# Attention output copied out of PSUM by one ScalarE operation per half head, with GpSimd moving the parts between partitions

## The chip, the cores and the metric

The kernel runs on one core of a Trainium2 chip. The metric is the device time of one execution in microseconds (us). Five engines matter: TensorE (PE in the profile, with its weight loads as a row of their own, PEld), VectorE (DVE), ScalarE (ACT), GpSimd (POOL), and SyncE (SP), which issues most of the DMAs. Each of them works through its own list of instructions in the order in which the program was built; an instruction that waits for a semaphore holds up all that stands behind it on its engine.

## The reference

A clustered attention over 2 batches, 8 heads, 768 positions and head dimension 64, followed by two layers of the form x @ w_in, an elementwise function, @ w_out:

```python
mask = q_assign[:, :, :, None] == k_assign[:, :, None, :]
scores = scale * np.matmul(q, k.transpose(0, 1, 3, 2))
scores = np.where(mask, scores, -1000000000.0)
scores = scores - np.max(scores, axis=-1, keepdims=True)
attn = np.exp(scores)
attn = attn / (np.sum(attn, axis=-1, keepdims=True) + 1e-09)
return np.matmul(attn, v).astype(np.float32)
...
x = np.ascontiguousarray(attn_out.transpose(0, 2, 1, 3)).reshape(B * S, H * D)
h = x @ w_in          # first layer: g = h * cos(h)
return (g @ w_out)    # the second layer has a piecewise quadratic in place of h * cos(h)
```

`q_assign` and `k_assign` are the index of the nearest of 16 centroids per head.

## The kernel before

All matrix products are made from two parts per operand, a rounded high part and the remainder, so that products keep nearly full fp32 accuracy. The work has two stages.

**Attention (to about 285 us).** There are 8 pairs (a batch and two neighbouring heads). A pair has four units (i, h, hf): head h of the pair, half hf of the 768 queries; they run in the order h0 hf0, h0 hf1, h1 hf0, h1 hf1. A unit has six slots. In each slot PE transposes a 128-row piece of the probabilities (`p_transpose`, L499, into one of three PSUM banks with the tag "t"), ACT copies it as its high part `phi` (L502), DVE subtracts for the low part `plo` (L507), PE makes scores eight slots ahead (L453, L456), DVE takes the row maximum `nm` (L462), ACT the exponential `p` (L471), and PE multiplies phi and plo with the values (`p_v`, L517 and L518) into `o`, the only PSUM bank of its kind. `o` holds 128 partitions: 64 of the product with the high part of V, 64 of that with the low part.

When a unit's sixth product is issued, `o_parts` follows: ACT copies the half of `o` that is called main into the tile `xt0` and the other half into `xt1` (L531, two operations of 64 x 384). Both heads of a pair share these two tiles, on 64 partitions each. After a unit with h = 1, `finish` follows two slots later: PE transposes the reciprocals `rb` of the softmax sums into a bank `r` (L541, tag "t" too), GpSimd adds xt0 and xt1 (L543), DVE multiplies the sum by r (L544), and GpSimd makes the two parts `xh` (L547) and `xl` (L551) that the layers read. So each pair has two finishes, one for each hf; below they are called the first and the second finish of a pair.

`inverse` makes the reciprocals of a unit: GpSimd adds a small number to `den` (L481), DVE inverts (L482), and GpSimd spreads each of three columns over 64 columns of `rb` (L486, three operations that multiply a tile `ones` by the column).

Beside this runs `prep_pair`, which prepares the pair after the next in small steps between slots: transposes of q and k (L322), their parts on GpSimd (L294, L295), products with the centroids (`pd`), the assignment to a centroid on DVE and GpSimd (`eq` L382 on DVE, times `desc` L383 on GpSimd, `mx` L388 and `dots` L390 on DVE), the two parts of V (`vv`, L403 and L404 on GpSimd), a transpose of `dots` on PE (`po`, L410, tag "t"), and its copy `oht` on ACT (L430). Its end falls beside the second finish of pairs 0 to 5.

**The two layers (from about 285 us).** PE runs long products (L652 to L654); the other engines apply the elementwise functions and split the weights into parts (`convert_chunk`, L144 to L160).

What sets the order: functions are put off by a number of slots with `later`, and a scheduler then places the instructions of each engine; the order on an engine is fixed when the kernel is built.

## Time and profile before

| what | value |
|---|---|
| time, median of 3 runs | 826.47 us (824.32 to 827.69) |
| the profiled execution's own time | 821.31 us |
| its span | 819.5 us |
| PE, DVE, ACT, POOL busy | 97%, 77%, 51%, 33% of the span |
| granted TensorE clock | 1.00 (full speed) |

The span is what the instructions cover; 1.8 us of the execution lie around it. PE is busy nearly all of the span, but its records overlap, so a busy PE is not a PE at its peak; waits are read from the idle time ahead of single instructions. A row of the timeline gives the start, the length, the engine, the line, what is written from what, the shape, a count where neighbours are merged, and in square brackets the idle time of the engine before it and what ended it.

### The profile page before, as it was taken

To read this page: it belongs to the slowest core of one execution; us is meant where nothing else is said; L and a number is where in the kernel's file an instruction comes from. 1 tells how busy PE (TensorE), PEld (TensorE's weight loads), DVE (VectorE), ACT (ScalarE), POOL (GpSimd) and SP (SyncE) were. 2 spreads that over 40 slices of the span, in tenths; PEclk is the share of its full clock that TensorE was granted. 3 is DMA by queue.
4 is the path that set the end of the run, shared out by engine and by line. 5 is a ranking of instruction groups with operands and counts; after the bars stand their busy time and mean duration, and the time that the engine had idled before them with its cause. 6 is when DMAs were issued, how large, how long until landed. Compare 5 with 4: busy or idle time off the path is not lost.

```text
span 819.5 us, 11332 instructions
## 1 busy us (share of the span) xinstructions
PE 798.6 (97%) x4042; PEld 665.8 (81%) x4043; DVE 633.6 (77%) x957; ACT 417.1 (51%) x794; POOL 270.4 (33%) x442
## 2 busy tenths in 40 slices
PE   7899999999999999999999999999999999999998
PEld 4788888988888887888888888888888888888886
DVE  5779899899898686787878778887876987755552
ACT  3788888897889764444343424223434233222220
POOL 3356655577553241222211211442231122111110
PEclk9999999999999999999999999999999999999999
DMA  7847556446540002222131222121122121000012
GB/s 145 192 89 155 142 121 166 101 107 137 137 89 33 1 15 89 102 70 85 51 104 52 103 58 97 52 88 67 52 59 96 56 89 62 1 1 0 14 50 92
DMA packets 48183, 65.97 MB, mean 80 GB/s; under 512 B 27904, under 2 KB 32640, under 8 KB 48128
## 3 DMA queue, kind: packets, MB, share of 16 engines
q1 hardware_dynamic: 46432, 64.83, 29.0%
q10 hardware_dynamic: 1696, 0.43, 0.3%
q8 instruction: 32, 0.52, 0.3%
q14 instruction: 23, 0.19, 0.1%
HBM read 43.02 MB, written 3.15 MB: 56 GB/s over the span
## 4 chain that ended last, share of the span: by engine, by line
PE 62%; DVE 1%; ACT 1%; POOL 1%; issue 0%; POOLq 0%
PE y L654 11%; PE y L653 11%; PE y L652 11%; PE h L653 10%; PE h L654 10%; PE h L652 10%; DVE gl L614 0%; DVE r L622 0%; POOL gh L610 0%; DVE g L627 0%; ACT L623 0%; ACT r L623 0%; DVE w L160 0%; ACT n L621 0%; ACT wx L144 0%
## 5 line engine op out<-in xcount | busy, mean ns | idle before, releaser
L610 POOL TENSOR_SCALAR gh<-g 128x512 fp32r<-128x512 f32 x96 | 70.8, 738 | 292.4 <-DVE g L641 165.3
L653 PE MATMUL h<-xl,w 128*128 128x512 f32 x384 | 151.5, 395 | 0.0
L652 PE MATMUL h<-xh,w 128*128 128x512 f32 x384 | 151.5, 395 | 0.0
L654 PE MATMUL h<-xh,w 128*128 128x512 f32 x384 | 151.4, 394 | 0.0
L507 DVE TENSOR_TENSOR plo<-pt,phi 128x384 fp32r<-128x384 f32 x192 | 99.8, 548 | 16.9 <-ACT phi L502 15.6
L502 ACT ACTIVATE phi<-pt 128x384 fp32r<-128x384 f32 x192 | 91.2, 493 | 21.0 <-PE pt L499 19.1
L637 ACT ACTIVATE p<-h,mone 128x512 f32<-128x512 f32 x48 | 33.0, 688 | 134.4 <-DVE m L636 134.0
L499 PE MATMUL pt<-ident,p 128*128 128x128 f32 x576 | 96.7, 278 | 4.3 <-DVE plo L507 2.8
L462 DVE TENSOR_REDUCE nm<-s 128x1 f32<-128x768 f32 x96 | 90.7, 946 | 6.9 <-PE s L456 6.3
L471 ACT ACTIVATE p<-s,nm 128x768 f32<-128x768 f32 x96 | 86.8, 904 | 12.8 <-DVE nm L462 12.5
L614 DVE TENSOR_TENSOR gl<-g,gh 128x512 fp32r<-128x512 f32 x96 | 71.1, 741 | 20.0 <-POOL gh L610 15.0
L654 PEld LDWEIGHTS h<-xh,w 128*128 128x128 f32 x384 | 71.9, 187 | 17.6
L653 PEld LDWEIGHTS h<-xl,w 128*128 128x128 f32 x384 | 71.9, 187 | 17.5
L652 PEld LDWEIGHTS h<-xh,w 128*128 128x128 f32 x384 | 71.9, 187 | 17.5
L144 ACT ACTIVATE wx<-wraw 128x1024 f32<-128x1024 f32 x32 | 36.4, 1138 | 95.6 <-DMA wraw<-in_moe_w_in_dram 35.8
L453 PE MATMUL s<-st,st 128*128 128x384 f32 x192 | 78.7, 411 | 4.2 <-ACT p L471 3.6
L499 PEld LDWEIGHTS pt<-ident,p 128*128 128x128 f32 x576 | 69.2, 140 | 15.1 <-DVE plo L507 3.1
L654 PE MATMUL y<-gh,w 128*128 128x512 f32 x192 | 74.9, 390 | 1.2 <-DVE w L160 1.2
L691 DVE TENSOR_TENSOR acc<-y,acc 128x512 f32<-128x512 f32 x72 | 49.3, 685 | 33.5 <-PE y L654 33.5
L653 PE MATMUL y<-gl,w 128*128 128x512 f32 x192 | 74.9, 390 | 0.0
L653 PE MATMUL y<-w,gh 128*128 128x512 f32 x192 | 74.9, 390 | 0.0
L652 PE MATMUL y<-gh,w 128*128 128x512 f32 x192 | 74.8, 390 | 0.0
(118 smaller groups left out, 1641.7 us busy)
## 6 DMA issues: line engine op xcount, KB each, us to landing
wraw<-in_moe_w_in_dram SPq DMA_DIRECT2D x16, 1024.0 KB, 5.2
wraw<-in_moe_w_out_dram SPq DMA_DIRECT2D x16, 1024.0 KB, 4.9
st<-t SPq DMA_DIRECT2D x24, 192.0 KB, 4.4
st<-th SPq DMA_DIRECT2D x9, 384.0 KB, 3.9
st<-tl SPq DMA_DIRECT2D x18, 192.0 KB, 4.1
st<-th SPq DMA_DIRECT2D x18, 192.0 KB, 4.2
nat<-in_q_dram SPq DMA_DIRECT2D x8, 384.0 KB, 5.3
natv<-in_v_dram SPq DMA_DIRECT2D x8, 384.0 KB, 4.7
```

The source lines that it names most:

```text
L453: nc.tensor.matmul(s[:, step, :HS], qt[:, 0, cols], kt[:, 0, kc], start=True, stop=False)
L462: nc.vector.tensor_reduce(nm, s[:, :, :HS], AX.XY, ALU.max, negate=True)
L471: nc.scalar.activation(p, s[:, :, :HS], AF.Exp, bias=nm, accum_out=dens[u][:, jj, 0:1])
L499: nc.tensor.transpose(ps[:, jj * P:(jj + 1) * P], p[:, kt * P:(kt + 1) * P], ident)
L502: nc.scalar.activation(hi, ps, AF.Copy)
L507: nc.vector.tensor_tensor(lo, ps, hi.bitcast(F32), ALU.subtract)
L610: nc.gpsimd.tensor_scalar(hi, g, 1.0, 0.0, ALU.mult, ALU.add)
L614: nc.vector.tensor_tensor(lo, g, hi.bitcast(F32), ALU.subtract)
L652: nc.tensor.matmul(o, lh, rh, start=first, stop=False)
L653: nc.tensor.matmul(o, lh, rl, start=False, stop=False)
L654: nc.tensor.matmul(o, ll, rh, start=False, stop=last)
L691: nc.vector.tensor_tensor(a, po, a, ALU.add)
```

## The change

`o_parts` copies the whole of `o`, 128 x 384, in one ACT operation into a tile of its own, `xt0` for h = 0 and `xt1` for h = 1. The parts of the two heads then lie on opposite partitions. After the second head, three GpSimd operations of 64 x 384 bring them together: one takes partitions 64 to 127 of head 0's tile to partitions 0 to 63 of a third tile `xt2`, one takes partitions 0 to 63 of head 1's tile to partitions 64 to 127 of `xt2`, and one takes partitions 0 to 63 of head 0's tile to the same partitions of head 1's tile. The sum in `finish` then reads `xt1` and `xt2`. `inverse` writes all three columns in one GpSimd operation, 128 x 192, from a broadcast of `den`, and the tile `ones` is gone.

```diff
-            for jj in range(HJ):
-                nc.gpsimd.tensor_scalar(rb[(i, hf)][:, jj, h], ones, den[:, jj, 1:2], 1.0,
-                                        ALU.mult, ALU.mult)
+            nc.gpsimd.tensor_scalar(
+                rb[(i, hf)][:, :, h], den[:, :, 1].unsqueeze(2).to_broadcast([P, HJ, D]),
+                1.0, 0.0, ALU.mult, ALU.add)
...
-            if h == 0:
-                xt[(i, hf)] = [ap.tile([P, HS], F32, tag=f"xt{n}", bufs=2,
-                                       name=f"xt{n}_{i}_{hf}") for n in range(2)]
-            for t, rows in zip(xt[(i, hf)], (main, other)):
-                nc.scalar.activation(t[main], o[rows], AF.Copy)
+
+            t = ap.tile([P, HS], F32, tag=f"xt{h}", bufs=2, name=f"xt{h}_{i}_{hf}")
+            xt.setdefault((i, hf), []).append(t)
+            nc.scalar.activation(t, o, AF.Copy)
             if h == 1:
+                t0 = xt[(i, hf)][0]
+                t2 = ap.tile([P, HS], F32, tag="xt2", bufs=1, name=f"xt2_{i}_{hf}")
+                xt[(i, hf)] = (t, t2)
+                for dst, rows, src in ((t2, main, t), (t2, other, t0), (t, other, t0)):
+                    src = src[rows] if dst is t else src[main if rows is other else other]
+                    nc.gpsimd.tensor_scalar(dst[rows], src, 1.0, 0.0, ALU.mult, ALU.add)
                 later(2, finish, i, hf)
```

The scheduler places the new operations. GpSimd's list around the second finish of pair 2 before the change, from the end of the first finish (`xl`) on; `vv` are the parts of V of the pair that is being prepared, and the row that adds two `xt` tiles is the sum of this finish:

```order
L551 TENSOR_TENSOR xl<-xt_2_0_1592,xh 128x384
L383 TENSOR_TENSOR eq_1909<-eq_1909,desc 128x384
L403 TENSOR_SCALAR vv_2037<-natv_1526 128x6x64 x2
L404 TENSOR_TENSOR vv_2037<-natv_1526,vv_2037 128x6x64
L543 TENSOR_TENSOR xt_2_1_1713<-xt_2_1_1713,xt_2_1_1714 128x384
L404 TENSOR_TENSOR vv_2037<-natv_1526,vv_2037 128x6x64
L481 TENSOR_SCALAR den_1944<-den_1944 128x3
```

and the same place with the change (the line numbers differ there: L535 are the three copies, L546 is the sum, and L381, L401 and L402 are L383, L403 and L404 of before):

```order
L554 TENSOR_TENSOR xl<-xt_2_0_1835,xh 128x384
L535 TENSOR_SCALAR xt_2_1_1961<-xt_2_1_1695 64x384
L381 TENSOR_TENSOR eq_1891<-eq_1891,desc 128x384
L401 TENSOR_SCALAR vv_2019<-natv_1512 128x6x64 x2
L535 TENSOR_SCALAR xt_2_1_1961<-xt_2_1_1959 64x384
L402 TENSOR_TENSOR vv_2019<-natv_1512,vv_2019 128x6x64
L535 TENSOR_SCALAR xt_2_1_1959<-xt_2_1_1695 64x384
L402 TENSOR_TENSOR vv_2019<-natv_1512,vv_2019 128x6x64
L546 TENSOR_TENSOR xt_2_1_1959<-xt_2_1_1959,xt_2_1_1961 128x384
L479 TENSOR_SCALAR den_1924<-den_1924 128x3
```

One copy stands ahead of `eq`, two stand between the `vv` operations, and the sum moved behind the second low part of V. The second finishes of pairs 0 and 3 read like this one. In pairs 4 and 5 the two high parts of V stand ahead of `eq`, in both kernels, and the rest is the same. In pair 1 the sum stood behind both low parts of V already, and only the copies come ahead of it.

DVE's list at the same place, with the change:

```order
L505 TENSOR_TENSOR plo_3_1970<-pt_3_1965,phi_3_1969 128x384
L505 TENSOR_TENSOR plo_4_1982<-pt_4_1977,phi_4_1981 128x384
L547 TENSOR_TENSOR xt_2_1_1961<-xt_2_1_1959,r_1_1996 128x384
L388 TENSOR_TENSOR dots_1789<-eq_1891,mx_1890 128x384
L480 RECIPROCAL den_1924<-den_1924 128x3
L460 TENSOR_REDUCE nm_2040<-s_1984 128x1
```

Nothing moved here: before the change the same operations stand in the same places (DVE's row 207 is the product of this finish in both), `dots` right behind the product `xt<-xt,r`.

## Rows read from the trace of the kernel before

**Rows 1.** One stretch: busy us (instructions) of PE, PEld, DVE, ACT, POOL; clock, DMA.

```profile
125.00:165.00 40.00, 38.76 (x265) 35.80 (x265) 35.52 (x62) 33.03 (x74) 24.31 (x45) 1.00 0.54 126
```

**Rows 2.** Groups by line and shape: busy us, mean ns | idle before, releaser.

```profile
L531 ACT ACTIVATE xt<-o 64x384 f32<-64x384 f32 x64 | 31.0, 484 | 2.9 <-PE o L518 2.1
...
L330 ACT ACTIVATE t<-ptq 128x384 f32<-128x384 f32 x24 | 11.9, 495 | 0.6 <-PE ptq L322 0.4
...
L486 POOL TENSOR_SCALAR rb<-ones,den 128x64 f32<-128x64 f32 x96 | 30.1, 332 | 5.6 <-DVE den L482 5.6
...
L305 POOL TENSOR_SCALAR st<-th 64x768 fp32r<-64x768 f32 x2 | 1.7, 828 | 0.2
```

**Rows 3.** Waits from 40 to 285 us: who for whom, us, times, longest.

```profile
PEld o L517 <- ACT xt L531: 6.9, 16, 0.7
...
PE o L517 <- ACT xt L531: 2.2, 7, 0.4
```

**Rows 4.** Timeline of GpSimd, second finish of pair 2.

```profile
131.27 1.00 POOL L383 TENSOR_TENSOR eq<-eq,desc 128x384 f32<-128x384 f32 x1 [0.49 <-DVE eq L382]
132.24 0.99 POOL L403 TENSOR_SCALAR vv<-natv 128x384 fp32r<-128x384 f32 x2
133.20 1.01 POOL L404 TENSOR_TENSOR vv<-natv,vv 128x384 fp32r<-128x384 f32 x1
134.18 1.01 POOL L543 TENSOR_TENSOR xt<-xt,xt 128x384 f32<-128x384 f32 x1
135.15 1.01 POOL L404 TENSOR_TENSOR vv<-natv,vv 128x384 fp32r<-128x384 f32 x1
```

**Rows 5.** DVE and PE there: the product, `dots`, and `po` that reads it.

```profile
135.22 0.56 DVE L544 TENSOR_TENSOR xt<-xt,r 128x384 f32<-128x384 f32 x1
135.69 0.88 DVE L390 TENSOR_TENSOR dots<-eq,mx 128x384 f32<-128x384 f32 x1
...
136.75 0.50 PE L410 MATMUL po<-ident,dots 128*128 128x128 f32 x3
...
139.27 0.44 PE L453 MATMUL s<-st,st 128*128 128x384 f32 x1 [0.21 <-ACT p L471]
```

**Rows 6.** Second finish of pair 1: GpSimd's sum, DVE, PE.

```profile
101.11 1.01 POOL L543 TENSOR_TENSOR xt<-xt,xt 128x384 f32<-128x384 f32 x1
...
102.16 0.56 DVE L544 TENSOR_TENSOR xt<-xt,r 128x384 f32<-128x384 f32 x1 [0.78 <-POOL xt L543]
102.63 0.55 DVE L390 TENSOR_TENSOR dots<-eq,mx 128x384 f32<-128x384 f32 x1
...
103.32 0.52 PE L410 MATMUL po<-ident,dots 128*128 128x128 f32 x3 [0.29 <-DVE den L482]
...
105.87 0.44 PE L453 MATMUL s<-st,st 128*128 128x384 f32 x1 [0.21 <-ACT p L471]
```

**Rows 7.** Second finish of pair 4: GpSimd's sum, DVE's product, `po`.

```profile
199.26 1.00 POOL L543 TENSOR_TENSOR xt<-xt,xt 128x384 f32<-128x384 f32 x1
...
200.63 0.54 DVE L544 TENSOR_TENSOR xt<-xt,r 128x384 f32<-128x384 f32 x1
...
202.43 0.49 PE L410 MATMUL po<-ident,dots 128*128 128x128 f32 x3
```

**Rows 8.** First finish of pair 2, and PE's wait ahead of the second.

```profile
124.73 1.00 POOL L543 TENSOR_TENSOR xt<-xt,xt 128x384 f32<-128x384 f32 x1 [2.89 <-ACT xt L531]
...
127.78 0.54 DVE L544 TENSOR_TENSOR xt<-xt,r 128x384 f32<-128x384 f32 x1
...
132.46 0.44 PE L517 MATMUL o<-phi,vv 128*128 128x384 f32 x1 [0.39 <-ACT xt L531]
```

**Rows 9.** The end of attention: the last finish, then the first layer's first ACT.

```profile
284.40 0.98 ACT L531 ACTIVATE xt<-o 64x384 f32<-64x384 f32 x2 [1.12 <-PE o L518]
...
285.46 1.02 POOL L543 TENSOR_TENSOR xt<-xt,xt 128x384 f32<-128x384 f32 x1 [0.70 <-ACT xt L531]
...
288.81 0.60 ACT L621 ACTIVATE n<-h 128x512 int32<-128x512 f32 x1 [3.42 <-POOL xl L551]
```

More of the change, by code (lines that the diff above doesn't have):

```diff
@@ L74, in attention_moe_moe @@
         nc.gpsimd.memset(desc[:, c:c + 1], float(C - c))
-    ones = cpool.tile([P, D], F32, name="ones")
-    nc.gpsimd.memset(ones, 1.0)
     ohscale = cpool.tile([P, 1], F32, name="ohscale")
```

## The prediction, made blind

> **What bounds the kernel now.** I read the busy times by stretch first, then the waits, then the timeline around the copies, and last the chain of waits at the end of attention. From 125 to 165 us PE is busy 38.76 of 40 us [rows 1], so in the attention stage PE sets the pace and all that another engine can give back is PE's idle time: 1.24 us in 40, some 7.6 us from 40 to 285 us. DVE and ACT, at 35.5 and 33.0 of 40, are close behind, and each of the two stalls PE now and then. The two layers behind attention are not touched by the edit. So the question is which of PE's waits the edit takes away, and whether it puts others in their place.
>
> The wait that the edit aims at is there: PE's next product into `o` waits for ACT to have copied `o` out, 16 times for 6.9 us on the weight load ahead of it, of which 2.2 us in 7 cases show as idle time of the matmuls themselves [rows 3]. At 132.46 us PE sat idle 0.39 us for it [rows 8].
>
> A second thing matters more. GpSimd's sum (L543) at the second finish of a pair is followed by DVE's product (L544) almost at once: the sum of pair 2 ends at 134.18 + 1.01 = 135.19 us [rows 4], the product starts at 135.22 [rows 5]. DVE had just come to it, so nothing is lost today, but nothing is left either. Behind the product on DVE stands `dots`, and PE's transpose `po` waits for `dots`: it starts at 136.75, 0.18 us after `dots` ends. PE works its list in order.
>
> **What ACT gives back.** 64 copies of 0.484 us go; 32 copies of 128 x 384 come, which I price by the same shape copied from PSUM at L330, 0.495 us [rows 2]. ACT is relieved of 31.0 - 15.8 = 15.2 us, and `o` is free 0.49 us sooner per unit. By the paragraph above that is worth between 0 and 7.6 us, since PE cannot gain more than it idles. The waits named for these copies are the nearer rows: 2.2 us as seen on the matmuls, 6.9 us on the loads. Part of them lies between `eq` and `po` of a second finish, as the one at 132.46 does; there the GpSimd chain below sets when `po` runs, and an earlier `o` only makes PE wait longer for it. I take 2.5 us, a little above what the matmuls show, because ACT's exponentials behind a copy come sooner too.
>
> **What GpSimd gets.** The broadcast of the reciprocals: 96 operations of 0.332 us go, 32 of 128 x 192 come. I have no row of that shape; 128 x 64 takes 0.33 us and 128 x 384 about 0.50 us (two in 0.99 us, [rows 4]), so it lies between, some 0.35 us, and each unit frees some 0.6 us of GpSimd. This is off the path. What it hides is the copy that now stands ahead of `eq`: that copy fits in that 0.6 us plus the 0.49 us for which GpSimd waited there [rows 4], so `eq` does not move. Without that cover it would cost another 0.5 us per second finish.
>
> The copies: 48 of 64 x 384. No copy between partitions on GpSimd is in the trace. An operation over 64 partitions takes 0.83 us for 768 columns [rows 2], one over 128 partitions 0.50 us for 384 [rows 4], so the count of columns sets the time and not that of partitions, and a copy takes 0.50 us; below it could be 0.33 us, as for 64 columns [rows 2], above 1.0 us, as for two-input work of 384 columns [rows 4]. I take 0.50 us, from the row of the same columns.
>
> **First finishes.** Two copies stand ahead of the sum: +1.0 us, and 0.1 us for each of the two waits of one GpSimd operation for the one before (an estimate, from the 0.08 us by which the sum of the last finish starts after ACT's end at 285.38 [rows 9]), less the 0.49 us by which ACT is sooner: +0.7 us. The sum of pair 2 ends at 125.73 and DVE's product starts at 127.78 [rows 8], so 2.05 us are left there; GpSimd had idled 2.89 us before. Hidden.
>
> **Second finishes of pairs 0, 2, 3.** Between `eq` and the sum GpSimd now has two copies more (2 x 0.50) and the second low part of V, which before stood behind the sum (0.98 us, from 133.20 to 134.18 [rows 4]): +1.98 us. DVE's place for the product has not moved, and the 0.03 us of slack are kept as the delay of the signal. So the product of pair 2 starts at 137.20 in place of 135.22, and DVE stands idle in front of it for about 2 us with `dots`, the reciprocal, the next `nm` and `plo` behind it. How `po` follows when PE is already waiting is seen in pair 1, where both low parts of V are ahead of the sum today: DVE idles 0.78 us for the sum, PE idles 0.29 us, and `po` starts 103.32 - 102.16 = 1.16 us after the product [rows 6]. Then `po` of pair 2 starts at 138.36 in place of 136.75: +1.6 us. Three pairs: 4.8 us.
>
> **Pair 1.** Only the copies come in, each now followed at once by one that needs its result: 1.0 us and 0.2 us for these waits. DVE waits already, so all of it is added: 1.2 us.
>
> **Pairs 4 and 5.** The same +1.98 us on GpSimd; its sum of pair 4 ends at 200.26, DVE came at 200.63 [rows 7], so the product moves to 200.26 + 1.98 + 0.03 = 202.27, and `po` to 203.43 from 202.43: +1.0 us. Pair 5 reads alike. Together 2.0 us.
>
> **Where it goes.** Is that stall made good later? From `po` to the next place where PE waits for ACT's exponential it is 2.52 us in pair 2, where `po` did not wait (136.75 to 139.27 [rows 5]), and 2.55 us in pair 1, where it did (103.32 to 105.87 [rows 6]). The pipeline starts from `po` alike in both cases; the delay is carried on whole. Loss at second finishes: 4.8 + 1.2 + 2.0 = 8.0 us.
>
> The Trainium skill, "SBUF — State Buffer", section Who interferes with whom, says that a DVE operation with two SBUF inputs and a GpSimd operation that reads SBUF shut each other out for the whole instruction. `dots` took 0.88 us beside a low part of V and 0.55 us alone [rows 4 to 6]; blocked to 136.16 it would have ended at 136.71, and it ended at 136.57, so the trace agrees nearly. With the change no GpSimd work is left beside `dots`, which is why 1.16 us (pair 1) and not 1.53 us (pair 2) is the distance that I use; by the latter the loss would be 1.1 us larger in the first three.
>
> **The end.** The last finish has no cover: ACT ends 0.49 us sooner, but three copies come ahead of the sum, one of them behind `xl` of the finish before: the sum starts about 1.1 us later than 285.46, and the first layer's `n` on ACT, which waits for the last `xl` [rows 9], with it. The chain that ended last runs through this `n`. +1.0 us.
>
> **Sum.** 8.0 - 2.5 + 1.0 = +6.5 us: 827.8 us for an execution like the profiled one (821.31 us). That execution is 0.6% below the median of the runs, 826.47 us; against the median I say 833.0 us, 0.8% more. A measurement of this kernel can tell some 0.5%, 4.1 us, from no change.
>
> **The rivals.**
> *The stall is swallowed.* DVE comes to its product later than today for another reason, or the ACT time given back shortens PE's two waits behind `po`, so that half the 8.0 us is regained. For it: DVE and ACT are both nearly full. Against it: the equal distances in pairs 1 and 2. It decides once DVE arrives over 1 us later than today. 4.0 - 2.5 + 1.0 = +2.5 us, 829.0 us: no change to tell.
> *The edit does what it is for.* The gain is the 6.9 us of the loads and GpSimd's extra work finds cover everywhere, at +1.0 us at the end: -5.9 us, 820.6 us, faster. It needs the product to stand 2 us later on DVE than it does today, and the list of DVE is unchanged there. Against it also that some of the 6.9 us lies beside matmuls that still ran.
> *The copies cost double*, 1.0 us each, like two-input work: then 2 x 0.5 us more at six second finishes, 1.5 us more at the end: +6.5 + 7.5 = +14, 840.5 us. Against it the rows for one input. The Trainium skill, "GPSIMD Engine Reference", section Engine selection, advises against GpSimd for elementwise work, about half as fast as DVE for two inputs, but near line rate for one; the rows for one and for two inputs, 0.50 and 1.0 us, agree with that.
>
> **How the numbers follow.** Forecast 0.60, swallowed 0.20, what it is for 0.10, double 0.10. The forecast's own spread: copies of 0.33 us take some 2 us off, a gain of 6 us in place of 2.5 takes 3.5 off, a gain of nothing adds 2.5; so 829 to 837 us, and some 0.07 of its 0.60 ends within 0.5% of before. Slower 0.63, same 0.26, faster 0.11. The range reaches from inside the second case to just short of the double price: 825.5 to 838.5 us, with about 0.1 out on either side.
>
> **What would show it.** Right: an idle time of DVE of 1.6 to 2 us before its product at six places, ended by GpSimd's sum; `po` on PE waiting for DVE over 1 us at the same six; the wait of PE for the copy of `o` much smaller; GpSimd's copies at 0.5 us; the first layer starting some 6 us later. Wrong: if DVE's idle time there is short, or if PE's idle time elsewhere in the stage shrinks by as much as `po` adds. Then attention ends as early as before and the edit is worth nothing or a gain.

## The result, and the profile after

The changed kernel takes 832.96 us (median of 4 runs, 832.28 to 837.25) against 825.39 us for the kernel before on the same chip (823.11 to 827.69). The ratio is 1.011 with a 95% interval of 1.008 to 1.0141: slower by 6.6 to 11.6 us, 9.1 us in the middle (the two medians are 7.6 us apart). The forecast was 833.0 us.

The profiled execution took 833.6 us, 12.3 us more than the one of before. I split its span at two marks in both traces: the end of the last `o` matmul of the first unit, and that of the last unit.

| stretch | before | after | difference |
|---|---|---|---|
| start, to the end of the first unit | 39.69 us | 43.57 us | +3.9 |
| attention, first to last unit | 244.68 us | 251.45 us | +6.8 |
| the two layers, to the end of the span | 535.13 us | 536.78 us | +1.65 |

The first of the three isn't the edit's. A stretch's row has its length, then busy us (instructions) of PE, PEld, DVE, ACT, POOL, the granted clock, DMA share and GB/s:

```profile
9.60:19.80 10.20, 10.20 (x40) 7.60 (x40) 6.21 (x16) 0.98 (x2) 4.75 (x5) 0.50 0.99 192
214.40:217.80 3.40, 3.40 (x16) 3.27 (x15) 2.77 (x5) 2.99 (x9) 0.36 (x2) 0.50 0.28 74
```

From 9.6 to 19.8 us TensorE ran at half its clock, the 1.2 GHz level. In the profiled execution of before it ran at 1.00 there. The kernel with the broadcast alone, below, has the same stretch at 0.50, its first unit ends at 43.43 us, and its time is that of the kernel before. So about 8.4 us of the profile's difference are the edit's. The second row is another such drop, inside attention; it comes back at the end.

In attention PE is no longer full. The stretch of [rows 1], with the edit:

```profile
125.00:165.00 40.00, 36.71 (x257) 34.29 (x256) 32.81 (x59) 29.60 (x66) 23.48 (x38) 1.00 0.65 149
```

PE 36.71 us in place of 38.76, ACT 29.60 in place of 33.03. The new operations, by line and shape (busy us, mean ns | idle before, releaser), cost what was put down for them:

```profile
L535 POOL TENSOR_SCALAR xt<-xt 64x384 f32<-64x384 f32 x48 | 25.3, 527 | 55.9 <-ACT xt L528 53.7
...
L528 ACT ACTIVATE xt<-o 128x384 f32<-128x384 f32 x32 | 15.9, 497 | 2.4 <-PE o L516 2.3
L483 POOL TENSOR_SCALAR rb<-den 128x192 f32<-128x192 f32 x32 | 11.3, 354 | 9.3 <-DVE den L480 9.3
```

ACT's copies went from 31.0 us [rows 2] to 15.9. And the waits from 40 to 292 us (us, times, longest) show both sides of the edit at once:

```profile
DVE xt L547 <- POOL xt L546: 15.3, 8, 2.6
...
PE po L408 <- DVE den L480: 10.3, 6, 1.9
...
PEld o L515 <- ACT xt L528: 1.5, 6, 0.4
...
PE o L515 <- ACT xt L528: 0.3, 1, 0.3
```

The wait that the edit aimed at fell from 6.9 us on the loads and 2.2 us on the matmuls [rows 3] to 1.5 and 0.3. In its place PE waits 10.3 us for `po`, in six places, where it waited 0.29 us once [rows 6]. The rows name `den` for it, because DVE's reciprocal of `den`, right behind `dots`, is what ended last before `po` started; what `po` reads is `dots`.

One such place, GpSimd at the second finish of pair 2, to be held beside [rows 4]:

```profile
135.97 1.01 POOL L381 TENSOR_TENSOR eq<-eq,desc 128x384 f32<-128x384 f32 x1
136.94 0.99 POOL L401 TENSOR_SCALAR vv<-natv 128x384 fp32r<-128x384 f32 x2
138.02 0.51 POOL L535 TENSOR_SCALAR xt<-xt 64x384 f32<-64x384 f32 x1
138.61 1.01 POOL L402 TENSOR_TENSOR vv<-natv,vv 128x384 fp32r<-128x384 f32 x1
139.59 0.51 POOL L535 TENSOR_SCALAR xt<-xt 64x384 f32<-64x384 f32 x1
140.07 1.00 POOL L402 TENSOR_TENSOR vv<-natv,vv 128x384 fp32r<-128x384 f32 x1
141.04 0.99 POOL L546 TENSOR_TENSOR xt<-xt,xt 128x384 f32<-128x384 f32 x1
```

GpSimd idles nowhere here for more than 0.1 us; the sum simply stands at the end of its list and starts 5.07 us after `eq`, where it was 2.91. DVE and PE at the same place, beside [rows 5]:

```profile
138.55 1.01 DVE L505 TENSOR_TENSOR plo<-pt,phi 128x384 fp32r<-128x384 f32 x2
142.06 0.55 DVE L547 TENSOR_TENSOR xt<-xt,r 128x384 f32<-128x384 f32 x1 [2.50 <-POOL xt L546]
142.54 0.55 DVE L388 TENSOR_TENSOR dots<-eq,mx 128x384 f32<-128x384 f32 x1
...
143.23 0.52 PE L408 MATMUL po<-ident,dots 128*128 128x128 f32 x3 [1.85 <-DVE den L480]
...
145.78 0.44 PE L451 MATMUL s<-st,st 128*128 128x384 f32 x1 [0.21 <-ACT p L469]
```

DVE comes to the product at 139.56 us and stands 2.50 us; `dots`, which has nothing to do with the sum, stands behind it; `po` follows 1.17 us after the product; 2.55 us later PE waits 0.21 us for ACT, exactly as before. Pair 1 and pair 4, beside [rows 6] and [rows 7]:

```profile
108.05 0.55 DVE L547 TENSOR_TENSOR xt<-xt,r 128x384 f32<-128x384 f32 x1 [2.61 <-POOL xt L546]
...
109.22 0.52 PE L408 MATMUL po<-ident,dots 128*128 128x128 f32 x3 [1.82 <-DVE den L480]
...
211.65 0.56 DVE L547 TENSOR_TENSOR xt<-xt,r 128x384 f32<-128x384 f32 x1 [1.76 <-POOL xt L546]
...
212.82 0.52 PE L408 MATMUL po<-ident,dots 128*128 128x128 f32 x3 [1.44 <-DVE den L480]
```

At a first finish, beside [rows 8], the same copies cost nothing: the sum is over at 131.29 us, and DVE comes to the product at 132.65 without having waited.

```profile
129.09 1.10 POOL L535 TENSOR_SCALAR xt<-xt 64x384 f32<-64x384 f32 x2 [2.90 <-ACT xt L528]
130.27 1.02 POOL L546 TENSOR_TENSOR xt<-xt,xt 128x384 f32<-128x384 f32 x1
...
132.65 0.54 DVE L547 TENSOR_TENSOR xt<-xt,r 128x384 f32<-128x384 f32 x1
```

The end of attention, beside [rows 9]: three copies between ACT's and the sum.

```profile
295.12 0.49 ACT L528 ACTIVATE xt<-o 128x384 f32<-128x384 f32 x1 [1.78 <-PE o L516]
295.84 1.69 POOL L535 TENSOR_SCALAR xt<-xt 64x384 f32<-64x384 f32 x3
297.62 1.02 POOL L546 TENSOR_TENSOR xt<-xt,xt 128x384 f32<-128x384 f32 x1
...
300.98 0.60 ACT L624 ACTIVATE n<-h 128x512 int32<-128x512 f32 x1 [5.36 <-PE h L657]
```

From the end of the last `o` matmul (295.02 us) to the first layer's `n` it is 5.96 us; before it was 288.81 - 284.37 = 4.44 us. PE doesn't stand still for this, as it has products of the first layer to run. It meets the delay once, at a product of the second layer that waits for the weight part `w`, which DVE makes 19 us behind `n` in both kernels; this is the only wait of its matmuls behind attention, before and after:

```profile
309.41 0.50 PE L654 MATMUL y<-gh,w 128*128 128x512 f32 x1 [1.17 <-DVE w L160]
...
321.76 0.50 PE L657 MATMUL y<-gh,w 128*128 128x512 f32 x1 [2.17 <-DVE w L158]
```

That is 1.0 of the 1.65 us. The rest is work on the other side of the mark: three of the first layer's products `h`, some 0.23 us each, ran ahead of the last `o` product before and run behind it now.

### The profile page after: what moved, and what is told of

It is laid out like the page before. It is cut to its first block, busy times and chain, and to the rows that moved or that the text cites. A ratio compares the mean times of both kernels' runs of the same rounds, so it can differ in the third digit from the quotient of the medians.

```text
span 831.8 us, 11292 instructions
## 1 busy us (share of the span) xinstructions
PE 800.6 (96%) x4043; PEld 671.0 (81%) x4043; DVE 631.3 (76%) x957; ACT 400.1 (48%) x762; POOL 278.0 (33%) x425
## 4 chain that ended last, share of the span: by engine, by line
PE 80%; DVE 5%; POOL 5%; ACT 4%; issue 3%; DMA 2%; SPq 1%; ACTq 0%; POOLq 0%; DVEq 0%
PE y L657 10%; PE y L656 10%; PE y L655 10%; PE h L657 10%; PE h L656 10%; PE h L655 10%; PE pt L497 5%; PE s L451 3%; PE s L454 2%; PE o L515 2%; PE o L516 2%; DVE plo L505 1%; POOL vv L402 1%; ACT p L469 1%; PE pd L351 1%
## 5 line engine op out<-in xcount | busy, mean ns | idle before, releaser
L500 ACT ACTIVATE phi<-pt 128x384 fp32r<-128x384 f32 x192 | 92.9, 501 | 28.4 <-PE pt L497 26.4
L656 PE MATMUL y<-w,gh 128*128 128x512 f32 x192 | 74.8, 390 | 0.0
L655 PE MATMUL y<-w,gh 128*128 128x512 f32 x192 | 74.7, 389 | 0.0
```

The source lines that it names most:

```text
L500: nc.scalar.activation(hi, ps, AF.Copy)
L655: nc.tensor.matmul(o, lh, rh, start=first, stop=False)
L656: nc.tensor.matmul(o, lh, rl, start=False, stop=False)
```

## The experiments

The theory: the loss is the *place* of the copies in GpSimd's list, ahead of a sum for which DVE waits with `dots` and so `po` behind it; ACT's shorter copy is a true gain beside it. The rivals, by the letters that the expectations use: A, ACT's 128-row form or the broadcast costs; B, the stalls are swallowed and the difference is the start's clock; C, the GpSimd work itself costs, wherever it stands; D, any time that DVE stands still ends up on PE. "In us" below is the ratio's excess times the median of the kernel before in the same comparison.

One number is taken from every trace: PE's time in the **six stretches** that hold a second finish beside a preparation, each from the end of one unit's last `o` matmul to that of the next, and in the rest of attention.

| kernel (one profiled execution each) | six stretches | rest of attention | ratio, 95% interval |
|---|---|---|---|
| before | 48.65 us | 196.03 us | 1 |
| changed | 57.93 | 193.52 | 1.011, 1.008 to 1.0141 |
| broadcast alone | 48.00 | 196.80 | 0.9999, 0.9981 to 1.0016 |
| GpSimd copies alone | 53.37 | 197.52 | 1.0076, 1.0053 to 1.0099 |
| one late copy more | 60.88 | 194.57 | 1.0173, 1.0141 to 1.0205 |
| product put off | 63.91 | 205.37 | 1.0354, 1.0317 to 1.039 |
| `dots` first | 54.75 | 195.13 | 1.0051, 1.0032 to 1.007 |
| head 0 alone | 48.11 | 195.00 | 0.9985, 0.9965 to 1.0004 |
| head 0 alone, V parts behind xl | 47.92 | 196.22 | 0.9998, 0.9979 to 1.0018 |
| V low parts behind the sum | 53.99 | 190.88 | 1.0044, 1.002 to 1.0069 |
| V parts behind the sum, last finish as before | 54.62 | 194.01 | 1.0019, 0.9999 to 1.004 |
| V parts behind xl | 45.48 | 193.05 | 0.9964, 0.9946 to 0.9982 |
| before, V parts behind xl | 48.08 | 196.41 | 0.999, 0.997 to 1.001 |
| V parts behind xl, pairs 6 and 7 by head 0 alone | 45.54 | 192.96 | 0.9917, 0.9892 to 0.9943 |

The rest holds the first units too, which depend on how the start went, so the six stretches are the firmer of the two.

### Parts of the edit

**The broadcast alone.**

```diff
 # on the kernel before
-            for jj in range(HJ):
-                nc.gpsimd.tensor_scalar(rb[(i, hf)][:, jj, h], ones, den[:, jj, 1:2], 1.0,
-                                        ALU.mult, ALU.mult)
+            nc.gpsimd.tensor_scalar(
+                rb[(i, hf)][:, :, h], den[:, :, 1].unsqueeze(2).to_broadcast([P, HJ, D]),
+                1.0, 0.0, ALU.mult, ALU.add)
```

> The kernel before with the single broadcast for rb alone (one GpSimd operation for three), ACT's copies as they were. Theory (the loss is the place of the two late copies in GpSimd's queue): there is no late copy, so the time is that of the kernel before, 0 to -1 us, po waits on TensorE no longer than 0.3 us, and DVE's product waits no longer than before (0.8 us at pair 1). Rival A (the broadcast or its place in the order costs by itself): +3 us or more.

Measured: 0.9999 (0.9981 to 1.0016), no po wait at all in attention. The broadcast is worth nothing and costs nothing that can be seen. And its profile has the slow start:

```profile
9.40:19.60 10.20, 10.15 (x39) 7.69 (x40) 6.30 (x16) 1.15 (x3) 4.76 (x5) 0.50 0.95 188
```

with a span of 823.3 us in place of 819.5, 3.7 of the 3.8 us ahead of the second unit, at an equal time over the runs. That settles the 3.9 us at the start: they belong to the execution, not to the edit.

**GpSimd copies without ACT's relief.** The copies write a tile onto itself; ACT keeps its two operations.

```diff
 # on the broadcast alone, in o_parts after ACT's copies
             if h == 1:
+                ta, tb = xt[(i, hf)]
+                for dst in (ta[other], tb[main], ta[main]):
+                    nc.gpsimd.tensor_scalar(dst, dst, 1.0, 0.0, ALU.mult, ALU.add)
                 later(2, finish, i, hf)
```

> The kernel before with the broadcast and with three GpSimd copies per finish that change nothing (64 rows x 384 onto themselves, two of them after the last ACT copy, ahead of the sum); ACT keeps its two copies for each half head. Theory (place in GpSimd's queue; ACT's shorter copy gives some 2.5 us back): the po waits of 1.4 to 1.9 us at the six second finishes are there, and without ACT's relief the time is before +8 to +13 us, at or above the changed kernel's +8. Rival A (ACT's 128-row copy or what it reorders is the cost): 0 to +2 us. Rival B (only stalls that are swallowed; the difference is the clock at the start): 0 to +2 us.

Measured: 1.0076, +6.3 us (4.4 to 8.1): below the theory's range, far above the rivals'. The po waits were there but smaller:

```profile
PE po L408 <- DVE dots L388: 2.9, 5, 0.7
...
PE po L408 <- DVE den L480: 1.2, 1, 1.2
```

The reason is in GpSimd's list of this kernel: the second low part of V stands behind the sum, as in [rows 4]. The copies alone, then, delay the sum by two copies, and DVE waits 1.12 us in pair 2 where the edit makes it 2.50. So the edit's stall has two halves: the copies, and the low part of V that came ahead of the sum with them. Copies that give ACT nothing cost 5.4 us in the six stretches against the broadcast alone, of which 4.1 us are po waits. Of the remaining 1.3 us, 1.0 lies ahead of them: counted from DVE's `eq`, PE comes to `po` 0.16 to 0.18 us later at each of the six places than in the broadcast alone. Why, this trace doesn't show.

**Head 0 alone.** Half of ACT's relief, and the one GpSimd copy is done long before the sum.

```diff
 # on the changed kernel, o_parts
+            if h == 0:
+                ta, tb = xt[(i, hf)]      # tiles as before
+                nc.scalar.activation(ta, o, AF.Copy)
+                nc.gpsimd.tensor_scalar(tb[main], ta[other], 1.0, 0.0, ALU.mult, ALU.add)
+            else:
+                for t, rows in zip(xt[(i, hf)], (main, other)):
+                    nc.scalar.activation(t[main], o[rows], AF.Copy)
+                later(2, finish, i, hf)
```

> The changed kernel with the new way for head 0 of a pair alone: one 128-row ACT copy and one GpSimd copy, which is long done when the sum comes; head 1 keeps two ACT copies, so nothing stands between ACT and the sum. Theory (place in the queue): no po wait over 0.3 us; half of ACT's relief is left, so before +0 to -2 us. Rival C (the extra GpSimd work itself, wherever it stands, slows DVE by their shared use of the memory or keeps GpSimd late): a third of the copies, so a third of the loss or more, +3 us. Rival A (ACT's 128-row form costs): half of the loss, +4 us.

Measured: 0.9985, -1.2 us (-2.9 to +0.3); no po wait at all. The theory's value, though in its profile 1.0 us of the gain lies behind attention (534.09 us in place of 535.13), where PE's wait for `w` is gone: the scheduler placed `w` 16.7 us behind `n` on DVE. Rivals A and C (+4 and +3 us) fall: a 128-row copy on ACT and GpSimd work that nobody waits for cost nothing that can be seen.

**One late copy more.**

```diff
 # on the changed kernel
                     nc.gpsimd.tensor_scalar(dst[rows], src, 1.0, 0.0, ALU.mult, ALU.add)
+                nc.gpsimd.tensor_scalar(t[main], t[main], 1.0, 0.0, ALU.mult, ALU.add)
```

> The changed kernel with one GpSimd copy more per finish, after the last ACT copy and ahead of the sum, that changes nothing (64 rows x 384 onto themselves). Theory: each sum comes 0.59 us later (0.51 and the step to the next instruction); the po waits grow to 2.4 us (pairs 0 to 3) and 2.0 us (pairs 4, 5), 3.5 us in sum, the last finish by 0.6, first finishes of pairs 0 to 5 stay hidden (0.28 to 1.47 us of slack, pair 0 over by 0.3): the changed kernel +4 us, before +11 to +14 us. Rival B (stalls are swallowed by slack elsewhere): the changed kernel +0 to +1 us.

Measured: 1.0173, +14.2 us (11.6 to 16.9), 5.2 us above the changed kernel by the two ratios. The sum is as expected, but not by the way expected: the scheduler put one low part of V back behind the sum in all but pair 1, so `po` waited 1.8 us in pairs 0, 2 and 3 and 1.4 us in pairs 4 and 5, no longer than with two copies, and 10.5 us in all for 10.3. Where the order stayed, in pair 1, `po` waited 2.38 us in place of 1.82, close to the 0.59 us of a copy. The six stretches are 3.0 us longer all the same, and the clock fell in three of them, where it fell in one of the changed kernel's: those of pairs 0 and 3, with a drop, took 10.12 and 10.16 us, that of pair 2, without one, 9.24, where the changed kernel took 9.32. The end of the last unit to the end of the span takes 1.9 us more, with a fourth drop in it. So the value is luck, and as a dose for the single wait the run serves in pair 1 alone. B falls by the two runs above: the start's clock costs the runs nothing (0.9999), and copies without relief cost 6.3 us, not 0 to 2.

### What stands behind whom

**Putting the product off.** A first try at taking the product out of DVE's way: the transposes of `rb`, the product and `xh` three slots later.

```diff
 # on the changed kernel, finish
+            nc.gpsimd.tensor_tensor(t1, t1, t2, ALU.add)
+            later(3, product, i, hf, t1, t2)
+
+        def product(i, hf, t1, t2):
             r = ps_t.tile([P, HS], F32, tag="t", name=f"r{i}_{hf}")
...
-            nc.gpsimd.tensor_tensor(t1, t1, t2, ALU.add)
             nc.vector.tensor_tensor(t2, t1, r, ALU.mult)
```

> The changed kernel with the product on DVE, the transposes of rb ahead of it and the rounding behind it issued three slots later; all copies and the sum stay where they are. Theory (DVE waits for the sum with dots of the next pair behind it, and po and TensorE behind these): dots now stand ahead of the product, the 10.3 us of po waits vanish, and the time is before +0 to -3 us, as ACT's relief is left. Rivals A and C (the copies cost as work, on ACT, on GpSimd or by contention): it stays at +6 to +9 us. What it may cost by itself: the transposes move on TensorE, and the PSUM buffer of r is asked for at another place.

Measured: 1.0354, +29.1 us (26.1 to 32.1). A miss by both. The po waits did go, but DVE now ran on to the next thing that it needs from GpSimd, the `den` behind the same sum. At the second finish of pair 2:

```profile
146.81 0.18 DVE L480 RECIPROCAL den<-den 128x3 f32<-128x3 f32 x1 [3.68 <-POOL den L479]
```

and the transposes, which hold both copies of `rb` longer, made GpSimd wait 38.2 us for PE in all. PE stood 18.0 us in six places, ahead of these transposes, for DVE's `plo`. The wait went up, not away. The edit moved too much at once to say more.

**`dots` first.** The same aim with less moved: at the second finishes only DVE's product is placed behind `dots`.

```diff
 # on the changed kernel, shortened: finish keeps (i, hf, t1, t2, r) of a second finish; in prep_pair
                 nc.vector.tensor_tensor(dv, eq, mb, ALU.is_equal)
+                if held:                      # the product, in this place of DVE's list
+                    product(*held.pop())
```

> The changed kernel with dots of the next pair ahead of the product on DVE at the second finishes of pairs 0 to 5; GpSimd's queue, with the late sum, stays. Theory (the sum costs only through what stands behind the waiting product): po no longer waits, 10.3 us go; DVE still loses some 2 us at the product, which the row maxima and the low parts of P behind it take over in part, so before -2 to +4 us. Rival D (any 2 us that DVE stands still end up on TensorE, whatever stands behind): another wait on DVE takes po's place and it stays at before +6 to +9 us. The order on TensorE and DVE changes a little elsewhere too.

Measured: 1.0051, +4.2 us (2.6 to 5.8): half the loss is back, half not, between the theory and rival D. In four of six places `po` waits no longer, and PE waits 1.5 to 1.7 us soon after instead (PE's `pt` for DVE's product, 6.4 us in 4: both use the PSUM banks of the tag "t"). In the other two something new shows:

```profile
141.30 2.67 DVE L388 TENSOR_TENSOR dots<-eq,mx 128x384 f32<-128x384 f32 x1
141.60 1.00 POOL L405 TENSOR_TENSOR vv<-natv,vv 128x384 fp32r<-128x384 f32 x1
142.56 0.98 POOL L548 TENSOR_TENSOR xt<-xt,xt 128x384 f32<-128x384 f32 x1
...
144.11 0.52 PE L411 MATMUL po<-ident,dots 128*128 128x128 f32 x3 [1.37 <-DVE dots L388]
```

`dots` took 2.67 us beside an unbroken row of GpSimd work, in place of 0.55: it ended 0.43 us after GpSimd's sum, as if it had run only then. In the other of the two it took 2.21 us. So moving `dots` ahead of the product trades a wait in the list for a wait inside the instruction. The Trainium skill, "SBUF — State Buffer", section Who interferes with whom, says that a DVE operation with two SBUF inputs, as `dots` is, and GpSimd's reads shut each other out; this trace agrees, and shows that DVE can lose several GpSimd instructions in a row.

**The V parts out of the way.** Three kernels move V parts in GpSimd's list; the second changes the last finish too. In the first the two low parts of V are queued behind the sum of the second finish:

```diff
 # on the changed kernel, shortened; behind(x): placed on GpSimd behind instruction x
                 nc.gpsimd.tensor_scalar(hi, tv[:, h], 1.0, 0.0, ALU.mult, ALU.add)
-                nc.gpsimd.tensor_tensor(lo, tv[:, h], hi.bitcast(F32), ALU.subtract)
+                with behind(last_sum):
+                    nc.gpsimd.tensor_tensor(lo, tv[:, h], hi.bitcast(F32), ALU.subtract)
```

> The changed kernel with one thing moved: the two V low parts of a pair (0.97 us each on GpSimd) are queued behind the sum of the second finish instead of ahead of it. No other engine's order changes; the work is the same. Theory (the loss is the queue ahead of the sum): the sum starts 1.9 us sooner at the second finishes of pairs 0 to 5, DVE's product waits 0.6 us or less instead of 1.75 to 2.6, the po waits fall from 10.3 us to under 1, and the time is before +0.5 to -3 us, ACT's relief being left. Rival C (the copies' work or contention, wherever they stand): it stays at before +6 to +9 us.

Measured: 1.0044, +3.6 us (1.6 to 5.7): 5.4 us of the 9.1 are regained by moving two operations, which C excludes, but the time isn't that of before or better. As expected DVE's product waits 0.64 to 0.69 us and not at all in pairs 4 and 5, and the po waits fall to 1.3 us. What I had not seen is who stands behind the sum: GpSimd's `den`, for which DVE's reciprocal waits.

```profile
136.57 2.29 POOL L408 TENSOR_TENSOR vv<-natv,vv 128x384 fp32r<-128x384 f32 x2
...
139.17 0.18 DVE L486 RECIPROCAL den<-den 128x3 f32<-128x3 f32 x1 [1.17 <-POOL den L485]
```

In the second, all four V parts are behind the sum, and the very last finish gets its head 1 by two ACT copies.

```diff
 # on the changed kernel, shortened
+                with behind(last_sum):
                     nc.gpsimd.tensor_scalar(hi, tv[:, h], 1.0, 0.0, ALU.mult, ALU.add)
                     nc.gpsimd.tensor_tensor(lo, tv[:, h], hi.bitcast(F32), ALU.subtract)
...
+            if i == len(pairs) - 1 and hf == 1 and h == 1:
...
+                for t, rows in ((ta, main), (tb, other)):
+                    nc.scalar.activation(t[main], o[rows], AF.Copy)
```

> The changed kernel with all four V parts of a pair queued behind the sum of the second finish, and with head 1 of the very last finish by two ACT copies as before, so that no copy stands between ACT and the last sum. Theory: at the second finishes only the two copies (1.2 us) are left ahead of the sum and DVE's product no longer waits; po waits gone; the end gives back 1.2 us: before -2 to -5 us, better than either kernel. Rival C: before +5 to +8 us.

Measured: 1.0019, +1.6 us (-0.1 to 3.3). A miss. The product waits nowhere at the second finishes, `po` twice for 0.4 us, and the six stretches are still 54.62 us, because the same happens with the double length:

```profile
141.25 2.28 POOL L408 TENSOR_TENSOR vv<-natv,vv 128x384 fp32r<-128x384 f32 x2
...
143.84 0.18 DVE L486 RECIPROCAL den<-den 128x3 f32<-128x3 f32 x1 [2.15 <-POOL den L485]
...
145.38 0.55 PE L503 MATMUL pt<-ident,p 128*128 128x128 f32 x3 [1.29 <-DVE plo L511]
```

GpSimd's list holds three things for which DVE waits, `eq`, the sum and `den`; the V parts cost wherever they stand ahead of one of them. So in the third they go behind `xl`, where GpSimd idles, and nothing else moves but the issue of the next load of V, which comes behind them; the lists of PE, DVE and ACT are those of the changed kernel, instruction by instruction:

```diff
 # on the changed kernel, x_lo of a second finish, shortened
-            nc.gpsimd.tensor_tensor(lo, x32, hi.bitcast(F32), ALU.subtract)
+            low = nc.gpsimd.tensor_tensor(lo, x32, hi.bitcast(F32), ALU.subtract)
+            with behind(low):
+                v_parts()
```

> The changed kernel with all four V parts of a pair queued on GpSimd behind xl of the second finish, that is behind the sum, den and xh as well; nothing else moves, on no engine. With the V parts just behind the sum, the trace showed DVE's reciprocal waiting 2.15 us (1.17 us with the two low parts alone) for GpSimd's den behind them, and TensorE waiting 1.29 us (0.74 us) for low parts of P behind that. Theory (in-order queues alone: whoever is ahead on GpSimd of something that DVE waits for costs its own length): here nothing that anyone waits for is behind the V parts, so no DVE wait over 0.3 us at the second finishes, no po wait over 0.4 us, no pt wait over 0.5 us behind them; ACT's relief of 3 us is left against 1.7 us at the end: before -4 to 0 us. Rival C (the copies' work and contention): before +2 to +5 us, new waits in other places.

Measured: 0.9964, -3.0 us (-4.4 to -1.5). GpSimd and DVE at the second finish of pair 2, with both late copies in their place:

```profile
130.10 1.10 POOL L542 TENSOR_SCALAR xt<-xt 64x384 f32<-64x384 f32 x2
131.28 1.01 POOL L553 TENSOR_TENSOR xt<-xt,xt 128x384 f32<-128x384 f32 x1
132.52 0.54 DVE L554 TENSOR_TENSOR xt<-xt,r 128x384 f32<-128x384 f32 x1
132.78 0.20 POOL L486 TENSOR_SCALAR den<-den 128x3 f32<-128x3 f32 x1 [0.49 <-ACT p L476]
...
136.22 1.97 POOL L405 TENSOR_TENSOR vv<-natv,vv 128x384 fp32r<-128x384 f32 x2
138.90 0.51 POOL L542 TENSOR_SCALAR xt<-xt 64x384 f32<-64x384 f32 x1 [0.70 <-ACT xt L535]
```

The sum is over 0.23 us before DVE wants it, `den` waits for ACT and not for GpSimd, and the V parts end with 0.70 us to spare. The same instructions as in the changed kernel, on the same engines, are 1.5% apart by their order on an engine that is busy a third of the time. C falls with this. The control on the kernel before:

```diff
 # on the kernel before, x_lo of a second finish: the same lines
+            with behind(low):
+                v_parts()
```

> Control: the kernel before with its four V parts behind xl of the second finish, nothing else moved. Theory: with no copy ahead of the sum there was almost no wait to take away (one po wait of 0.29 us, one wait of DVE for the sum of 0.78 us), so before +0 to -1.5 us, and what the changed kernel gains by the same move comes from the queue that the edit made. Rival E (the V parts are simply in a better place there, whatever the edit): as large a gain as the changed kernel's, before -5 us or more.

Measured: 0.999 (0.997 to 1.001). Without the copies the move is worth nothing that can be seen, so the 12 us that the changed kernel gained by it were the queue that the edit had made.

### How much ACT's relief is worth

**Pairs 6 and 7 by head 0 alone**, the rest as with the V parts behind xl. There is no preparation beside these, but the sum of a finish waits for two late copies all the same, and the last one ends the stage.

```diff
 # on the V parts behind xl, o_parts
+            late = i >= len(pairs) - 2
+            if late and h == 1:
+                for t, rows in zip(xt[(i, hf)], (main, other)):
+                    nc.scalar.activation(t[main], o[rows], AF.Copy)
+                later(2, finish, i, hf)
+                return
...
+            if late:                          # tb: the second tile, as before
+                nc.gpsimd.tensor_scalar(tb[main], t[other], 1.0, 0.0, ALU.mult, ALU.add)
```

> As the run with the V parts behind xl, and pairs 6 and 7, which have no preparation of a later pair beside them, take the new way for head 0 alone (head 1 by two ACT copies, no late GpSimd copy). Theory: DVE's waits of 0.8 to 0.9 us at the finishes of pairs 6 and 7 go, and the end gives back 1.2 to 1.7 us: before -2 to -6 us. Rival C: before +1 to +4 us.

Measured: 0.9917, -6.8 us (-8.9 to -4.7), 817.33 us against 824.0: better than both kernels. The gain over the run before it shows behind attention: 534.07 us from the last `o` matmul to the end, in place of 536.71. There `n` comes 1.4 us sooner, and PE's wait of 2.09 us for `w` is gone, as `w` stands 16.7 us behind `n` on DVE in place of 19.5. The kernel before has that wait too (1.17 us), so some 1 us of the 6.8 comes from where the scheduler placed `w` and not from the copies. At the end of attention the last sum starts 0.08 us after ACT's second copy (279.93 + 0.98 = 280.91), with no copy of GpSimd's between:

```profile
279.93 0.98 ACT L536 ACTIVATE xt<-o 64x384 f32<-64x384 f32 x2 [1.19 <-PE o L523]
280.99 1.01 POOL L563 TENSOR_TENSOR xt<-xt,xt 128x384 f32<-128x384 f32 x1 [0.76 <-ACT xt L536]
```

**Head 0 alone, V parts behind xl.**

```diff
 # on head 0 alone, x_lo of a second finish
+            with behind(low):
+                v_parts()
```

> The run with the new way for head 0 alone, and with the V parts behind xl in addition: no late copy, V parts out of the way, half of ACT's relief. The full relief was worth about 6 us in the attention (238.5 us from unit 0 to unit 31 against 244.7 us before) once nothing else stood in the way, the half one 1.6 us with the V parts where they were. Theory F (the relief counts for head 0 and head 1 alike, and the rest of the half one was lost to the V parts beside the sum): attention 241.5 to 242 us, before -2.5 to -4 us. Theory G (it counts where two ACT copies hold up the next o matmuls and scores on TensorE, which are the ones of head 1 beside the preparation, waits of 0.45 and 0.3 us): attention 243 us and before -0.5 to -2 us, as without moving the V parts.

Measured: 0.9998 (0.9979 to 1.0018), 244.1 us from the first to the last unit. Theory F falls. The time is next to G's range, with even less gained than it gave; the profile's 244.1 us hold a drop of the clock to 0.50 from 190.60 to 194.01 us, so the 1 us over G's 243 is not all the kernel's. So nearly all of the relief belongs to head 1's copies, or to these together with head 0's: a kernel with head 1 alone was not run. The waits speak for head 1. PE's matmuls still wait 2.4 us in 7 cases for its copies, where it was 2.2 us in 7 for all copies before [rows 3], and 0.3 us once for head 0's. At 135.06 us it is 0.45 us, where 0.39 stood before [rows 8].

## Why the prediction came true, step by step

**The clock and the median.** The forecast put 0.8% on the median; the ratio is 1.1% (0.8 to 1.41). That 832.96 us lies beside the 833.0 us of the forecast is luck: the kernel before took 825.39 us in this comparison and not 826.47, and the excess was 9.1 us and not 6.5. The profiled executions differ by 12.3 us, and 3.9 of these are no part of the edit.

**ACT, the copies and the broadcast**: 497, 527 and 354 ns where 495, 500 and 350 stood. The 15.2 us off ACT were 31.0 - 15.9 = 15.1. The copy ahead of `eq` and the first finishes of pairs 0 to 5 were hidden, as said; the slack left at these is 0.28 to 1.47 us.

**The second finishes.** The mechanism came as forecast, place by place: DVE waits for the sum, `dots` behind it, `po` behind that, 1.17 us after the product (1.16 stood there), with nothing made good before ACT's next exponential (2.55 us). DVE's idle time was to be about 2 us in pairs 0, 2 and 3 and was 2.50. What was off there is "DVE's place for the product has not moved": DVE's own `eq` takes 0.55 us where it took 1.09, so DVE comes half a microsecond sooner and waits that much longer. Pair 2, before and after:

```profile
130.10 1.09 DVE L382 TENSOR_TENSOR eq<-dots,mx 128x384 f32<-128x384 f32 x1
...
134.97 0.55 DVE L380 TENSOR_TENSOR eq<-dots,mx 128x384 f32<-128x384 f32 x1
```

This doesn't make `po` later. From the start of this `eq` to the product it is 7.09 us where it was 5.12, the 1.98 us of the working. Two small misses cancel in that: GpSimd's way from its `eq` to the sum grew by 2.16 us (5.07 for 2.91), and its `eq` came 0.17 us sooner behind DVE's (1.00 for 1.17). From `eq` to `po` it is 8.26 us where it was 6.65: 1.61 us for the 1.6 of the forecast. Taken so, `po` came 1.62 to 1.65 us later in pairs 0, 2 and 3, 1.16 in pair 1, 1.12 and 1.35 in pairs 4 and 5: 8.55 us in all, and 8.0 was forecast. PE's waits for `po` add up to 10.3 us because 0.29 us stood there before and PE, with less to wait for at `o`, comes to each 0.1 to 0.4 us sooner. The six stretches lost 9.3 us: these 8.55, and some 0.6 in pair 4 for a drop of the clock (last section).

**What ACT gives back.** Put at 2.5 us. Against before, the units outside the six stretches gained 196.03 - 193.52 = 2.5 us and the six lost 9.3 (48.65 to 57.93), so the term is right where it could show; without the three `h` products that changed sides it is 1.8 us. It is no measure of the relief: with the V parts out of the way the six stretches fall to 45.48 us, 3.2 us below before, and attention in all by 6.1 us, or 5.4 without those products, below the upper bound of 7.6 that PE's idle time set and not far from the 6.9 us of waiting loads [rows 3]. The loads' waits were the nearer price, not the matmuls'; what lay at the second finishes was eaten at the second finishes, as the prediction said of it: an earlier `o` only makes PE wait longer for `po`. Read so, the queue cost 57.93 - 45.48 = 12.5 us, and 10.3 of that are the `po` waits.

**The end.** Put at 1.0 us, measured 1.5 us at `n`, 1.0 us in PE's wait for `w` (2.17 for 1.17) and 1.65 us by the end of the span, with the `h` products. The three copies and their waits took 297.62 - 295.61 = 2.0 us from ACT's end to the sum, where 0.08 was before; from the end of the last `o` matmul the sum starts 1.5 us later, where 1.1 stood.

**Not seen**: at the two finishes of pair 6 and the first of pair 7, DVE waits 0.80 to 0.94 us for the sum, where it had 0.4 us to spare. At the first two nothing on PE waits for it, as no preparation stands behind. At the third PE waits 0.54 us, at 294.58 us, for the `plo` that stands behind the product.

So +9.3 - 2.5 + 1.65 = +8.4 us by the trace, and +6.5 us was forecast; over the runs +9.1 us (6.6 to 11.6) and +6.5. With the `h` products on one side the terms are 9.3 for 8.0, 1.8 for 2.5 and 1.0 for 1.0: each is near, and the largest miss, 1.3 us at the second finishes, is half a drop of the clock that the sum had no term for. Of the rivals, that the stall is swallowed fell with the long waits, the copies at double price with 527 ns. *The edit does what it is for* came true, at -3.0 us and not -5.9, in the kernel with the V parts behind xl, where the sum comes sooner and not, as its condition said, the product later.

One aside of the prediction is wrong: "no GpSimd work is left beside `dots`". At 142.70 us `xh` runs beside it. It costs `dots` nothing, which started 0.16 us ahead and keeps its 0.55 us, so the distance of 1.16 us held; `xh` took 0.76 us, where it takes 0.51 alone.

## What to carry to other kernels

An engine that is busy a third of the time isn't free: ask, for each thing put into its list, which instruction behind it another engine waits for, and what stands behind that waiting instruction in turn. When a wait is taken away, go down the same list to the next one, since here it moved from the sum to `den` before it was gone, and put the filler behind the last of them, where the trace shows the engine idle. A relief that a first measurement shows as a loss may be real: look at the stretches without the new wait for what it gives.

## What the hardware showed beside this

**The clock sometimes drops after a stall.** In the changed kernel the granted clock was 0.50, the 1.2 GHz level, from 214.39 to 217.81 us (the second row of stretches above). PE had just stood 1.44 us for `po` at 212.82 and 0.26 us more at 214.10. The unit around it took 10.38 us, the like one a pair later, with the same `po` wait and no drop, 9.75: some 0.6 us. The four longer waits before it and the equal one after it brought no drop. With all V parts behind the sum, PE's `pt` waited 1.27 to 1.29 us at four second finishes, and the clock fell, at 77.8 and 111.9 us, after the first two of them only. With one late copy more it fell after po waits of 1.82, 2.38 and 1.79 us, and not after those of 1.77, 1.37 and 1.36; a stretch with a drop took 0.9 us more there (10.12 and 10.16 us for 9.24). So a stall can be followed by a loss beyond its length, but not each time; what decides it these runs don't show.

**A DVE operation can be held for several GpSimd ones.** `dots` took 0.55 us where it started ahead of the GpSimd operation beside it, 0.88 us where one low part of V was under way [rows 5], and 2.67 us beside a copy, a low part and a sum in a row. Where it came first, the GpSimd operation was the one that took longer:

```profile
142.70 0.76 POOL L550 TENSOR_SCALAR xh<-xt 128x384 fp32r<-128x384 f32 x1 [0.39 <-DVE xt L547]
```

**Equal work can stand on either side of a mark.** The two layers take 534.0 us in the kernel with `dots` first and 536.8 us in the changed kernel, though both have the same last finish. Eleven `h` products, some 2.6 us, stand ahead of the last `o` product in the first and none in the second, and PE waits 1.7 us behind it in place of 2.2.

**Open**: why PE comes to `po` later with copies that give no relief, and how the relief divides between the two heads.
